# Constant tables built on chip, phi and one piece of w1 by other routes, in a fused windowed attention and soft mixture of experts

## The chip, the cores and the metric

The kernel runs on one core of a Trainium2 chip. The metric is device time in microseconds (us) of one launch. The program before was run eight times: median 183.81 us, 183.51 to 184.37. One execution was also profiled; its trace is what is read below.

## The reference

Two stages, in float32, with fixed random inputs:

```
q, k, v: (8 batches, 8 heads, 576 positions, 64)
scores = q @ k^T / 8
heads 0-3: position i sees i-31 .. i          ("plain")
heads 4-7: i sees i, i-4, i-8, .. i-124       ("dilated")
x = softmax(scores) @ v, as (4608 rows, 512 columns)

phi: (512, 32)   w1: (8, 512, 1024)   w2: (8, 1024, 512)
logits = x @ phi                               (4608, 32)
slot_input = softmax over rows(logits)^T @ x   (32, 512), 4 slots per expert
slot_out[e] = relu(slot_input[e] @ w1[e]) @ w2[e]
out = softmax over slots(logits) @ slot_out    (4608, 512)
```

The slots need all rows of x, so the second half can't begin before the attention of all batches has ended. The weights are 33.6 MB of the 62 MB that are read.

## The kernel before

The attention runs batch by batch. `prologue` (line 466) issues the first loads and clears tiles; then a loop over b runs `slot0(b)`, `slot1(b)`, `slot2(b)` (lines 528 to 601). The order inside them is the order on every engine: the whole body stands under a manual schedule, and each engine runs its instructions in that order, waiting at each for what it needs.

Loads. All big loads and all stores are issued by POOL (GpSimd)[...]. They are one queue: a load that waits for a free buffer, or a POOL copy that waits for VectorE, holds back all loads after it. q and k go to `raw` tiles (two buffers each, `load_qk`), v to `vs` tiles (`load_v`), one piece of w1 per slot to `w1t` (`load_w1`, 512 rows of an expert in two pieces, called by `weights`), and w2 near the end of the attention (`load_w2`). The program gives POOL's DMAs eight completion semaphores in turn, so the n-th DMA can't be issued before the (n-8)-th has landed.

Attention. VectorE transposes q and k out of `raw` (`qk_plain` line 237, `qk_dil` line 243). `emit_scores` (line 255) fills two PSUM tiles, `sa` and `sb`: first the bias by a product of `ident` with `masks` (line 276), then the scores on top (line 287); ScalarE takes the exponential (line 298). It runs three times a batch: g = 0 and 1 for plain heads (with the left-over part of the dilated ones in g = 1), g = 2 for the dilated ones. `order_v_plain` (line 179) brings v into row order by products with the one-hot matrices in `orders`, in the same PSUM tiles `sa` and `sb`; ScalarE copies most of it out (line 197), VectorE a small tail (line 202), and POOL and VectorE spread the dilated part (`spread_v`, lines 207 to 216). `emit_av` (line 306) multiplies with v, `emit_norm` (line 353) normalises on VectorE.

Mixture. One batch behind, `back_xT_plain`, `back_xT_dil` and `back_logits` (lines 376 to 417) transpose x, multiply with `phi4` (phi, four copies side by side) and put the exponentials into `ET`, a tile for all 4608 rows. `back_erow` and `back_u` (lines 419 to 461) sum the slot inputs into `UT`; `emask` clears rows that don't exist. After the loop: hidden layer (`hps`, line 645), its transposes (line 658), `slot_out` (line 677) for half of the 512 output columns at a time, and `combine` / `combine_full` (lines 693 and 724), which multiply `ET` with the slot outputs, scale by `rrow` on ScalarE or VectorE, and store through POOL. Experts 6 and 7 come last and in halves of columns, so that the first half of the columns can be stored while the second half of w2 is read.

Constants before: `make_masks`, `make_orders` and an identity are arrays in the program. `masks` (84 KB) and `ident` (32 KB) are read by two DMAs of SP, `orders` (128 KB) by one of POOL, all in the prologue; phi is read in rows of 32 values and copied four times by VectorE in `slot0(0)` (line 541). `slot0(0)` also clears `ET` (line 538).

Of the kernel before, what the change touches and what calls it, by code (L numbers as in the profile page):

```python
# [19 lines left out]
WINDOW = 32  # L20
DIL = 4
# [6 lines left out]
N_SLOTS = 32  # L28
FDIM = 1024
# [13 lines left out]
UNITS = 7  # L43
NH = DMODEL // 2
NSPLIT = 16


def make_masks():

    a = np.arange(128)[:, None]  # L50
    rel = np.arange(WQ)[None, :] - a
    plain = (rel >= 0) & (rel < WINDOW)
    rel = 32 + np.arange(LEFT)[None, :] - a
    left = (rel >= 0) & (rel < WINDOW) & (a < 48)
    m = [plain, plain[:, 0:TAIL]] + [left] * 5
    m = [np.where(x, 0.0, -60000.0) for x in m]
    ok = ((np.arange(128)[:, None] % 32) < LEFT) & np.ones((1, N_SLOTS), bool)
    m.append(ok)
    return np.ascontiguousarray(np.concatenate(m, axis=1).astype(np.float16))


def make_orders():

    a = np.arange(128)[:, None, None] % 32
    r = np.arange(DIL)[None, :, None]
    p = np.arange(128)[None, None, :]
    return np.ascontiguousarray((p == DIL * a + r).astype(np.float16).reshape(128, DIL * 128))


@with_exitstack  # L70
def kernel(
# [9 lines left out]
):  # L81
    nc = tc.nc

    mask_np = make_masks()
    masks_dram = nc.inline_tensor(mask_np, name="masks_d")
    orders_dram = nc.inline_tensor(make_orders(), name="orders_d")
    ident_dram = nc.inline_tensor(np.eye(128, dtype=np.float16), name="ident_d")


    consts = ctx.enter_context(tc.tile_pool(name="consts", bufs=1))  # L90
    masks = consts.tile([128, mask_np.shape[1]], FP16, name="masks")
    bias = (
        masks[:, None, 0:WQ].broadcast_to([128, 3, WQ]),
        masks[:, 0 : W1 + NLEFT],
# [57 lines left out]
    def load_qk(ti, b, groups=None):  # L152
        ten = (q, k)[ti]
        if (ti, b) not in raw:
            raw[(ti, b)] = raw_pool.tile([128, 2, PJ * D], FP16, name=f"raw{ti}_{b}", tag=f"raw{ti}")
        t = raw[(ti, b)]
        if groups is None:
            nc.gpsimd.dma_start(
                out=t, in_=ten[b].rearrange("(g h) (p j) d -> (h p) g (j d)", g=2, j=PJ)
            )  # L160
# [18 lines left out]
    def order_v_plain(b):  # L179
# [16 lines left out]
        for ab in range(2):  # L196
# [4 lines left out]
            if ab == 0:  # L201
# [2 lines left out]
                    in_=ps[0][0:TAIL, 0, 256:512].rearrange("p (h d) -> p h d", h=4),  # L204
                )

    def spread_v(b):
        sa, sb = vstage.pop(b)
        nc.vector.tensor_copy(  # L209
            out=vD[b % NV][:, :, :, 0:D], in_=sa[:, 4:8].rearrange("a h (r d) -> a h r d", r=DIL)  # L210
        )
        nc.gpsimd.tensor_copy(
            out=vL[b % NV][32 : 32 + LEFT, :, :, 0:D],
            in_=sb[0:LEFT, 4:8].rearrange("a h (r d) -> a h r d", r=DIL),
        )
        nc.gpsimd.tensor_copy(out=vL[b % NV][0:32, :, :, 0:D], in_=vD[b % NV][96:128, :, :, 0:D])  # L216

    def load_w1(e, i):
        src = moe_w1[e].rearrange("(c p) f -> p c f", p=128)
        nc.gpsimd.dma_start(out=w1t[e][:, 2 * i : 2 * i + 2, :], in_=src[:, 2 * i : 2 * i + 2, :])  # L220

    def load_w2(e, half=None):
        if half is None:
# [218 lines left out]
    def back_u(b):  # L442
        up = ring.tile([128, 5, N_SLOTS], FP32, name=f"u_{b}", tag="ring")
        er = er_t.pop(b)
        jobs = []
        for t in range(NT):
            n = 128 if t < 4 else TAIL
            for c in range(2):
                jobs.append((c, xp_t[b][0:n, t, 128 * c : 128 * c + 128], er[0:n, t, :]))
            jobs.append((4, ones[0:n, :], er[0:n, t, :]))  # L450
        for r in range(DIL + 1):
            for c in range(2):
                jobs.append((2 + c, xd_t[b][:, r, 128 * c : 128 * c + 128], er[:, NT + r, :]))
# [44 lines left out]

    def weights(b, g):
        if b < B - 2:  # L500
            if g == 1 or b > 0:
                load_w1(*next_w1.pop(0))
        elif b == B - 2:
            if g == 0:
                while next_w1:
                    load_w1(*next_w1.pop(0))
                load_w2(0)
                load_w2(1)
            else:
                slab_weights(4, "vs0", V_SLAB)  # L510
                load_w2(4)
        elif g == 0:
            raw_pool.release()
            pool = tc.alloc_tile_pool(name="w2b", bufs=1, side="right")
            late_pools.append(pool)
            for e in (2, 3):
                w2t[e] = pool.tile([128, 8, DMODEL], FP16, name=f"w2_{e}", tag=f"w2_{e}")
                load_w2(e)
        else:
            slab_weights(5, "vs1", V_SLAB)  # L520
            load_w2(5)
            slab_weights(6, "qk0", QK_SLAB)
            slab_weights(7, "v0", V_SLAB)
            for half in range(2):
                for e in HALVED:
                    load_w2(e, half)

    def slot0(b):
        att, b1, b2, b3 = b < B, b - 1 >= 0 and b <= B, 2 <= b < B + 2, b + 1 < B
        if att:  # L530
            qk_dil(1, b, 1)
            emit_scores(b, 0)
            if b + 2 < B:
                load_qk(0, b + 2)
                load_qk(1, b + 2)
            weights(b, 0)
        if b == 0:
            nc.vector.memset(ET, 0.0)
# [151 lines left out]

    psum_f = tc.alloc_tile_pool(name="psum_f", bufs=4, space=bass.MemoryType.PSUM)

    def combine(half, pair):
# [103 lines left out]
```

The softmax here doesn't subtract the row's maximum and nothing guards it: scores larger than these inputs give would overflow.

## Time and profile before

| | us |
|---|---|
| median of 8 runs | 183.81 |
| the profiled execution, its own time | 183.51 |
| its span, first to last instruction | 181.5 |
| busy: TensorE, VectorE, ScalarE, POOL | 143.8, 105.0, 89.8, 80.8 |
| 26 output DMAs, first issued at | 153.50 |

The span is shorter than the device time by about 2 us, which lie around it. Busy time of TensorE comes from matmuls that overlap, so it isn't work at full rate; the granted clock was 0.88 of full speed on average, with stretches at 0.5. In rows of the profile a line number is that of the kernel, `out<-in` are tiles, the number in front of "x" is how often; "idle before" is time in which the engine waited, and the arrow says for what. POOL's row of a DMA is only its issue; the transfer itself runs on the DMA engines.

### The profile page before, as it was taken

To read this page: it belongs to the slowest core of one execution; us is meant where nothing else is said; L and a number is where in the kernel's file an instruction comes from. 1 tells how busy PE (TensorE), PEld (TensorE's weight loads), DVE (VectorE), ACT (ScalarE), POOL (GpSimd) and SP (SyncE) were. 2 spreads that over 40 slices of the span, in tenths; PEclk is the share of its full clock that TensorE was granted. 3 is DMA by queue.
4 is the path that set the end of the run, shared out by engine and by line. 5 is a ranking of instruction groups with operands and counts; after the bars stand their busy time and mean duration, and the time that the engine had idled before them with its cause. 6 is when DMAs were issued, how large, how long until landed. Compare 5 with 4: busy or idle time off the path is not lost.

```text
span 181.5 us, 5521 instructions
## 1 busy us (share of the span) xinstructions
PE 143.8 (79%) x2448; PEld 86.8 (48%) x2448; DVE 105.0 (58%) x225; ACT 89.8 (50%) x161; POOL 80.8 (45%) x112
## 2 busy tenths in 40 slices
PE   3067989999999999999999999999879476786000
PEld 0034556557557557655746747757343253332000
DVE  2587797858767866865876976354041103599000
ACT  2044367667666765845748748745201104698000
POOL 7643644552551751541642814711101111997820
PEclk9999999999999997897899999985557967899655
DMA  5999999999999999999999999999999999999996
GB/s 81 195 205 216 197 210 205 212 209 203 213 209 203 213 210 204 211 211 201 213 209 202 212 211 211 218 213 218 212 213 215 204 195 171 335 398 409 408 408 153
DMA packets 32023, 41.00 MB, mean 226 GB/s; under 512 B 2144, under 2 KB 19680, under 8 KB 32000
## 3 DMA queue, kind: packets, MB, share of 16 engines
q0 software_dynamic: 31712, 40.54, 120.1%
q8 instruction: 19, 0.31, 0.6%
q1 hardware_dynamic: 288, 0.12, 0.3%
q14 instruction: 4, 0.03, 0.0%
HBM read 62.18 MB, written 9.44 MB: 395 GB/s over the span
## 4 chain that ended last, share of the span: by engine, by line
PE 42%; DMA 29%; issue 7%; POOL 7%; ACT 6%; DVE 3%; POOLq 0%
DMA w<-in_moe_w_dram 23%; PE lg L413 8%; PE o_p L344 7%; DMA raw<-in_q_dram 6%; PE sa L287 6%; ACT p L298 6%; PE sa L276 5%; PE sb L276 4%; PE u L455 3%; PE rd L394 2%; PE vb L188 2%; PE va L188 2%; POOL out_dram L719 2%; POOL out_dram L743 2%; PE rp L382 1%
## 5 line engine op out<-in xcount | busy, mean ns | idle before, releaser
L298 ACT ACTIVATE p<-sa 128x960 f16<-128x960 f32 (+2 forms) x24 | 21.4, 891 | 31.7 <-PE sb L287 31.1
L344 PEld LDWEIGHTS <-p 128*128 128x128 f16 (+2 forms) x544 | 19.9, 100 | 12.7 <-issue 8.6
L241 DVE STREAM_TRANSPOSE qk<-raw 128x576 uint32<-128x576 uint32 x16 | 20.0, 1250 | 5.7 <-DMA raw<-in_q_dram 4.2
L250 DVE STREAM_TRANSPOSE qk<-raw 128x320 uint32<-128x320 uint32 (+1 forms) x32 | 21.5, 677 | 0.3
L298 ACT ACTIVATE p<-sb 128x960 f16<-128x960 f32 (+2 forms) x24 | 21.2, 884 | 0.0
L216 POOL COPY v<-v 32x1024 f16<-32x1024 f16 x8 | 8.3, 1035 | 26.9 <-DVE v L209 22.2
L287 PE MATMUL sa<-qk 32*128 32x160 f16 (+4 forms) x416 | 16.0, 215 | 4.3 <-DVE qk L241 4.3
L287 PEld LDWEIGHTS <-qk 32*128 32x128 f16 x832 | 12.3, 98 | 14.2 <-issue 8.7
L413 PE MATMUL lg<-xTd,phi 128*128 128x288 f16 x32 | 18.3, 659 | 0.0
L276 PE MATMUL sa<-masks,ident 128*128 128x480 f16 (+2 forms) x48 | 14.2, 381 | 4.4 <-DMA ident<-ident_d 2.9
L344 PE MATMUL o_p<-v,p 128*128 128x65 f16 (+1 forms) x288 | 16.5, 203 | 0.7 <-ACT v L197 0.7
L232 POOL DMA_DIRECT2D w<-in_moe_w_dram x8 | 5.9, 743 | 24.9 <-DMA w<-in_moe_w_dram 20.8
L276 PEld LDWEIGHTS <-ident 128*128 128x128 f16 x96 | 9.2, 105 | 15.4 <-issue 8.7
L287 PE MATMUL sb<-qk 32*128 32x160 f16 (+4 forms) x416 | 16.1, 215 | 0.0
L276 PE MATMUL sb<-masks,ident 128*128 128x480 f16 (+2 forms) x48 | 14.6, 386 | 0.5 <-issue 0.3
L366 DVE TENSOR_TENSOR xp<-o_p,rc_p 128x448 f16<-128x448 f32 (+1 forms) x24 | 14.4, 602 | 0.8
L366 DVE TENSOR_TENSOR xd<-o_d,rc_d 128x448 f16<-128x448 f32 (+1 forms) x24 | 14.4, 602 | 0.8
L719 POOL DMA_DIRECT2D out_dram<-ot x16 | 11.3, 712 | 6.7 <-PE f L697 6.7
L220 POOL DMA_DIRECT2D w<-in_moe_w_dram x16 | 11.4, 711 | 4.4 <-DMA w<-in_moe_w_dram 2.1
L188 PE MATMUL va<-vs,orders 32*128 32x256 f16 (+1 forms) x96 | 12.1, 289 | 1.0 <-ACT p L298 1.0
L417 ACT ACTIVATE ET<-lg 128x288 f16<-128x288 f32 x16 | 6.6, 411 | 12.0 <-PE lg L413 11.8
L713 DVE TENSOR_TENSOR ot<-f,rrow 128x512 f16<-128x512 f32 x8 | 5.5, 688 | 11.9 <-PE f L697 11.8
(86 smaller groups left out, 268.0 us busy)
## 6 DMA issues: line engine op xcount, KB each, us to landing
w<-in_moe_w_dram POOLq DMA_DIRECT2D x16, 512.0 KB, 16.3
w<-in_moe_w_dram POOLq DMA_DIRECT2D x6, 1024.0 KB, 27.3
out_dram<-of POOLq DMA_DIRECT2D x10, 512.0 KB, 6.3
vs<-in_v_dram POOLq DMA_DIRECT2D x8, 512.0 KB, 13.2
out_dram<-ot POOLq DMA_DIRECT2D x16, 256.0 KB, 4.7
raw<-in_q_dram POOLq DMA_DIRECT2D x7, 576.0 KB, 14.6
raw<-in_k_dram POOLq DMA_DIRECT2D x7, 576.0 KB, 14.8
w<-in_moe_w_dram POOLq DMA_DIRECT2D x8, 256.0 KB, 23.2
```

The lines of the kernel that those rows point to most:

```text
L188: nc.tensor.matmul(o.rearrange("p (h d) -> p h d", h=4), l, st[:, 0:4, D * r : D * r + D], start=(r == 0), stop=(r == DIL - 1), skip_group ...
L216: nc.gpsimd.tensor_copy(out=vL[b % NV][0:32, :, :, 0:D], in_=vD[b % NV][96:128, :, :, 0:D])
L220: nc.gpsimd.dma_start(out=w1t[e][:, 2 * i : 2 * i + 2, :], in_=src[:, 2 * i : 2 * i + 2, :])
L241: nc.vector.transpose(out=dst, in_=src)
L250: nc.vector.transpose(out=o, in_=i)
L276: nc.tensor.matmul(sps[h // 2][:, h % 2, 0:n], ident, bias[g], start=True, stop=False, skip_group_check=True,)
L287: nc.tensor.matmul(sps[h // 2][:, h % 2, c0 : c0 + w], kt_[32 * h : 32 * h + 32, k0 : k0 + 128, tt], qt_[32 * h : 32 * h + 32, q0 : q0 + w ...
L298: nc.scalar.activation(out=pt, in_=sps[ab][:, :, 0:n], func=AF.Exp, scale=SCALE)
L344: nc.tensor.matmul(o[p0 : p0 + np_, n, :], l, rr, start=(k == 0), stop=(k == len(jobs) - 1), skip_group_check=True,)
L366: nc.vector.tensor_tensor(out=x.rearrange("p t (h d) -> p (t h) d", h=4)[0:nq, u0:u1, :], in0=o[0:nq, 0:n, 0:D], in1=rc[0:nq, 0:n, None].b ...
L413: nc.tensor.matmul(lp, phi4[:, kc].rearrange("p c s -> p (c s)"), rhs, start=(kc == 0), stop=(kc == 3))
L719: nc.gpsimd.dma_start(out=out[r0 : r0 + 256, NH * half : NH * half + NH].rearrange("(k p) n -> p k n", k=2), in_=ot,)
```

## The change

Seven edits:

1. `masks`, `ident` and `orders` are no longer read. VectorE sets `masks`, `ones` and a quarter of `orders` to constants; POOL cuts them to shape with affine selects, five after v's first load and one, for `orders`, after q of batch 1. VectorE copies the tail part of `masks` (ahead of the first `qk_plain`) and three quarters of `orders` (ahead of the first `qk_dil`).
2. `emask`'s last block comes from a row sum over `orders` instead of a column block of `masks`.
3. phi is read as 128 rows of 512 bytes, later in POOL's queue, and put in order by 16 one-hot products in batch 1 (`order_phi`), in the PSUM tiles of the scores; ScalarE copies the four-fold result to `phi4`.
4. Each piece of w1 is read as two neighbouring rows a partition (8 KB in one run) instead of two rows 128 apart. `back_u` takes every second column of x, so that slot inputs match.
5. 64 partitions of the first piece of w1 are read as float32 by SP and ACT, 8 DMAs of 8 partitions, into a part of `ET` that is still unused (`side_load`); POOL casts them to their place in `slot0(0)` (`side_cast`), and `ET` is cleared after it. POOL's own load of that piece has only the other 64 partitions.
6. Two pieces of w1 are issued in the prologue and one in `slot0(0)`, where there was none; later pieces move up.
7. The first pair of output blocks of half 0 is stored block by block (`combine_one`).

```diff
@@ kernel head
-    mask_np = make_masks()
-    masks_dram = nc.inline_tensor(mask_np, name="masks_d")
-    orders_dram = nc.inline_tensor(make_orders(), name="orders_d")
-    ident_dram = nc.inline_tensor(np.eye(128, dtype=np.float16), name="ident_d")
...
+    def order_phi():
+        ps = [psum_s.tile([128, 2, 512], FP32, name=f"phi{ab}", tag=f"s{ab}") for ab in "ab"]
+        for r in range(DIL):
+            for c in range(4):
+                nc.tensor.matmul(
+                    ps[c // 2][:, c % 2, 0:128].rearrange("p (u s) -> p u s", u=4),
+                    orders[32 * c : 32 * c + 32, r, :],
+                    phi_raw[32 * c : 32 * c + 32, r, None, :].broadcast_to([32, 4, N_SLOTS]),
+                    start=(r == 0),
+                    stop=(r == DIL - 1),
+                    skip_group_check=True,
+                )
+        for ab in range(2):
+            nc.scalar.copy(
+                out=phi4[:, 2 * ab : 2 * ab + 2].rearrange("p c u s -> p c (u s)"),
+                in_=ps[ab][:, :, 0:128],
+            )
...
+    SIDE_P = 64
+    side = ET[0:SIDE_P, 0 : 4 * FDIM].bitcast(FP32)
+
+    def side_load():
+        src = moe_w1[0, 0:256].rearrange("(p l) f -> p (l f)", l=2)
+        for n, p in enumerate(range(0, SIDE_P, 8)):
+            (nc.sync, nc.scalar)[n % 2].dma_start(out=side[p : p + 8], in_=src[p : p + 8])
+
+    def side_cast():
+        nc.gpsimd.tensor_copy(
+            out=w1t[0][0:SIDE_P, 0:2, :].rearrange("p l f -> p (l f)"), in_=side
+        )
+
     def load_w1(e, i):
-        src = moe_w1[e].rearrange("(c p) f -> p c f", p=128)
-        nc.gpsimd.dma_start(out=w1t[e][:, 2 * i : 2 * i + 2, :], in_=src[:, 2 * i : 2 * i + 2, :])
+        p0 = SIDE_P if (e, i) == (0, 0) else 0
+        nc.gpsimd.dma_start(
+            out=w1t[e][p0:128, 2 * i : 2 * i + 2, :].rearrange("p l f -> p (l f)"),
+            in_=moe_w1[e, 256 * i : 256 * i + 256].rearrange("(p l) f -> p (l f)", l=2)[p0:128],
+        )
@@ back_u
-                jobs.append((c, xp_t[b][0:n, t, 128 * c : 128 * c + 128], er[0:n, t, :]))
+                x = xp_t[b][0:n, t, :].rearrange("p (x l) -> p l x", l=2)
+                jobs.append((c, x[:, c, :], er[0:n, t, :]))
...
@@ prologue
         load_qk(0, 0, (0,))
         load_qk(1, 0, (0,))
-        nc.sync.dma_start(out=masks, in_=masks_dram.ap())
-        nc.sync.dma_start(out=ident, in_=ident_dram.ap())
+        side_load()
+        nc.vector.memset(masks, 0.0)
+        nc.vector.memset(ones, 1.0)
+        nc.vector.memset(orders[0:32], 1.0)
...
         load_qk(0, 0, (1,))
         load_qk(1, 0, (1,))
-        nc.gpsimd.dma_start(out=orders.rearrange("p r n -> p (r n)"), in_=orders_dram.ap())
         load_v(0)
-        nc.gpsimd.dma_start(out=phi_raw, in_=moe_phi.rearrange("(c p) s -> p c s", p=128))
+        left = masks[:, W1:].rearrange("p (u c) -> p u c", c=LEFT)
+        band = (
+            (ident, ones, [[1, 128]], 0, -1, ALU.is_equal, 0.0),
+            (masks[:, 0:WQ], masks[:, 0:WQ], [[1, WQ]], 0, -1, ALU.is_ge, MASKED),
+            (masks[:, 0:WQ], masks[:, 0:WQ], [[-1, WQ]], WINDOW - 1, 1, ALU.is_ge, MASKED),
+            (left, left, [[0, 5], [1, LEFT]], 32, -1, ALU.is_ge, MASKED),
+            (left, left, [[0, 5], [-1, LEFT]], -1, 1, ALU.is_ge, MASKED),
+        )
+        for dst, src, pattern, base, mult, op, fill in band:
+            nc.gpsimd.affine_select(
...
         load_qk(0, 1)
+        nc.gpsimd.affine_select(
+            out=orders[0:32],
...
         load_qk(1, 1)
         load_v(1)
+        nc.gpsimd.dma_start(out=phi_raw, in_=moe_phi.rearrange("(p l) s -> p l s", l=4))
+        for _ in range(2):
+            load_w1(*next_w1.pop(0))
+        nc.vector.tensor_copy(out=masks[:, WQ:W1], in_=masks[:, 0:TAIL])
         qk_plain(0, 0)
         qk_plain(1, 0)
-        nc.vector.memset(ones, 1.0)
         nc.vector.memset(emask, 1.0)
+        for i in range(1, 4):
+            nc.vector.tensor_copy(out=orders[32 * i : 32 * i + 32], in_=orders[0:32])
@@ weights
         if b < B - 2:
-            if g == 1 or b > 0:
-                load_w1(*next_w1.pop(0))
+            load_w1(*next_w1.pop(0))
@@ slot0
         if b == 0:
+            side_cast()
             nc.vector.memset(ET, 0.0)
             nc.vector.memset(siTm, 0.0)
-            nc.vector.tensor_copy(out=emask[:, NE - 1, :], in_=masks[:, W1 + NLEFT :])
+            nc.vector.tensor_reduce(
+                out=halves, in_=orders[:, 0, 0:TAIL], axis=mybir.AxisListType.X, op=ALU.add
+            )
             nc.vector.tensor_copy(
-                out=phi4, in_=phi_raw[:, :, None, :].broadcast_to([128, 4, 4, N_SLOTS])
+                out=emask[:, NE - 1, :], in_=halves.broadcast_to([128, N_SLOTS])
             )
...
         if att and b > 0:
             order_v_plain(b)
+        if b == 1:
+            order_phi()
...
+    def combine_one(half, blk):
+        fp = psum_f.tile([128, NH], FP32, name=f"f{half}_one{blk}", tag="f")
+        cols = slice(NH * half, NH * half + NH)
+        r0 = 128 * blk
+        nc.tensor.matmul(fp, ET[:, r0 : r0 + 128], so_sb[:, cols], start=True, stop=True)
+        ot = out_pool.tile([128, NH], FP16, name=f"oo{half}_{blk}", tag=f"oo{half}_{blk}")
+        if blk % 2 == 0:
+            nc.scalar.activation(out=ot, in_=fp, func=AF.Copy, scale=rrow[:, blk : blk + 1])
+        else:
+            nc.vector.tensor_scalar(
+                out=ot, in0=fp, scalar1=rrow[:, blk : blk + 1], scalar2=None, op0=ALU.mult
+            )
+        nc.gpsimd.dma_start(out=out[r0 : r0 + 128, cols], in_=ot)
+
     def combine(half, pair):
+        if half == 0 and pair == 0:
+            combine_one(half, 0)
+            combine_one(half, 1)
+            return
```

More of the change, by code (lines that the diff above doesn't have):

```diff
@@ L43 @@
 UNITS = 7
+MASKED = -60000.0
 NH = DMODEL // 2
 NSPLIT = 16
[L48 to L67, printed above, removed]
 @with_exitstack
@@ L82 @@
     nc = tc.nc
-    mask_np = make_masks()
-    masks_dram = nc.inline_tensor(mask_np, name="masks_d")
-    orders_dram = nc.inline_tensor(make_orders(), name="orders_d")
-    ident_dram = nc.inline_tensor(np.eye(128, dtype=np.float16), name="ident_d")
     consts = ctx.enter_context(tc.tile_pool(name="consts", bufs=1))
-    masks = consts.tile([128, mask_np.shape[1]], FP16, name="masks")
+    masks = consts.tile([128, W1 + NLEFT], FP16, name="masks")
+    halves = consts.tile([128, 1], FP32, name="halves")
     bias = (
@@ L452, in back_u @@
             for c in range(2):
-                jobs.append((2 + c, xd_t[b][:, r, 128 * c : 128 * c + 128], er[:, NT + r, :]))
+                x = xd_t[b][:, r, :].rearrange("p (x l) -> p l x", l=2)
+                jobs.append((2 + c, x[:, c, :], er[:, NT + r, :]))
         for i, (c, l, rr) in enumerate(jobs):
@@ L480, in prologue @@
         load_qk(1, 0, (1,))
-        nc.gpsimd.dma_start(out=orders.rearrange("p r n -> p (r n)"), in_=orders_dram.ap())
         load_v(0)
-        nc.gpsimd.dma_start(out=phi_raw, in_=moe_phi.rearrange("(c p) s -> p c s", p=128))
-        load_qk(0, 1)
+        left = masks[:, W1:].rearrange("p (u c) -> p u c", c=LEFT)
[8 more added lines that the diff above has]
+            nc.gpsimd.affine_select(
+                out=dst,
+                in_=src,
+                pattern=pattern,
+                base=base,
+                channel_multiplier=mult,
+                compare_op=op,
+                fill=fill,
+            )
+        load_qk(0, 1)
+        nc.gpsimd.affine_select(
+            out=orders[0:32],
+            in_=orders[0:32],
+            pattern=[[-1, DIL], [1, 128]],
+            base=0,
+            channel_multiplier=-DIL,
+            compare_op=ALU.is_equal,
+            fill=0.0,
+        )
         load_qk(1, 1)
         load_v(1)
+        nc.gpsimd.dma_start(out=phi_raw, in_=moe_phi.rearrange("(p l) s -> p l s", l=4))
+        for _ in range(2):
+            load_w1(*next_w1.pop(0))
+        nc.vector.tensor_copy(out=masks[:, WQ:W1], in_=masks[:, 0:TAIL])
         qk_plain(0, 0)
         qk_plain(1, 0)
-        nc.vector.memset(ones, 1.0)
         nc.vector.memset(emask, 1.0)
+        for i in range(1, 4):
+            nc.vector.tensor_copy(out=orders[32 * i : 32 * i + 32], in_=orders[0:32])
         for part in range(2):
@@ L537, in slot0 @@
         if b == 0:
+            side_cast()
             nc.vector.memset(ET, 0.0)
             nc.vector.memset(siTm, 0.0)
-            nc.vector.tensor_copy(out=emask[:, NE - 1, :], in_=masks[:, W1 + NLEFT :])
+            nc.vector.tensor_reduce(
+                out=halves, in_=orders[:, 0, 0:TAIL], axis=mybir.AxisListType.X, op=ALU.add
+            )
             nc.vector.tensor_copy(
-                out=phi4, in_=phi_raw[:, :, None, :].broadcast_to([128, 4, 4, N_SLOTS])
+                out=emask[:, NE - 1, :], in_=halves.broadcast_to([128, N_SLOTS])
             )
@@ L691 @@
     psum_f = tc.alloc_tile_pool(name="psum_f", bufs=4, space=bass.MemoryType.PSUM)
+    def combine_one(half, blk):
[9 more added lines that the diff above has]
+                out=ot, in0=fp, scalar1=rrow[:, blk : blk + 1], scalar2=None, op0=ALU.mult
+            )
+        nc.gpsimd.dma_start(out=out[r0 : r0 + 128, cols], in_=ot)
     def combine(half, pair):
+        if half == 0 and pair == 0:
+            combine_one(half, 0)
+            combine_one(half, 1)
+            return
         fp = psum_f.tile([128, 2, NH], FP32, name=f"f{half}_{pair}", tag="f")
```

## The prediction

> **What bounds the kernel now.** I read the page first: the slices by time, the DMA queues, the chain of waits.
>
> ```profile
> DMA  5999999999999999999999999999999999999996
> GB/s 81 195 205 216 197 210 205 212 209 203 213 209 203 213 210 204 211 211 201 213 209 202 212 211 211 218 213 218 212 213 215 204 195 171 335 398 409 408 408 153
> HBM read 62.18 MB, written 9.44 MB: 395 GB/s over the span
> ```
>
> GB/s counts bytes written. Loads are float32 cast to float16, so 207 written is about 414 read, the same flow as the output's 408. The transfers never rest between about 4 and 179 us, so bytes alone set a floor for the span. But the second limit is close. One-microsecond windows (span, then busy PE, PEld, DVE, ACT, POOL, then clock, DMA share, GB/s) show a slow start and, in the middle, a TensorE with no idle time:
>
> ```profile
> 2.00:3.00 1.00, 0.14 (x1) 0.13 (x2) 0.31 (x3) 0.02 (x1) 1.00 (x2) 1.00 0.81 105
> 3.00:4.00 1.00, 1.00 (x3) 0.30 (x2) 0.00 (x0) 0.00 (x0) 1.00 (x3) 1.00 0.77 115
> ...
> 61.00:62.00 1.00, 1.00 (x4) 0.26 (x3) 0.97 (x3) 1.00 (x2) 0.49 (x1) 1.00 1.11 218
> ```
>
> So attention, at about 13.7 us a batch, can't catch up on a late start. How late may it be? I went to the timeline of the tail (start, length, what; idle before it in brackets):
>
> ```profile
> 141.93 1.17 PE L681 MATMUL so<-w,hTm 128*32 128x256 f16 x36 [0.38 <-DVE hTm L662]
> 145.79 3.38 PE L681 MATMUL so<-w,hTm 128*32 128x256 f16 x64 [2.69 <-DMA w<-in_moe_w_dram]
> 149.81 0.29 PE L681 MATMUL so<-w,hTm 128*32 128x256 f16 x4 [0.65 <-DMA w<-in_moe_w_dram]
> 151.13 0.29 PE L681 MATMUL so<-w,hTm 128*32 128x256 f16 x4 [1.02 <-DMA w<-in_moe_w_dram]
> 153.50 4.91 POOL L719 DMA_DIRECT2D out_dram<-ot  x7 [6.73 <-PE f L697]
> ```
>
> These waits are the whole slack between compute and weights: 2.69 + 0.65 + 1.02 = 4.36 us. A compute chain later by more starts the output later by the rest. Last, the timeline of the start, for what starts the attention:
>
> ```profile
> 4.94 0.59 POOL L175 DMA_DIRECT2D vs<-in_v_dram  x1
> 5.71 1.26 DVE L241 STREAM_TRANSPOSE qk<-raw 128x576 uint32<-128x576 uint32 x1 [3.29 <-DMA raw<-in_q_dram]
> 7.85 0.71 POOL L158 DMA_DIRECT2D raw<-in_k_dram  x1 [0.85 <-DMA raw<-in_k_dram]
> 9.23 2.55 DVE L250 STREAM_TRANSPOSE qk<-raw 128x320 uint32<-128x320 uint32 x4
> 12.20 2.00 DVE L538 MEMSET ET<- 128x2336 uint32 x1 [0.41 <-issue]
> 16.77 1.25 DVE L241 STREAM_TRANSPOSE qk<-raw 128x576 uint32<-128x576 uint32 x1 [0.95 <-DMA raw<-in_q_dram]
> 17.87 0.40 DVE L202 CAST v<-va 64x256 f16<-64x256 f32 x1
> 18.32 1.01 PE L276 MATMUL sa<-masks,ident 128*128 128x512 f16 x2 [0.24 <-DVE v L202]
> 20.23 1.25 DVE L241 STREAM_TRANSPOSE qk<-raw 128x576 uint32<-128x576 uint32 x1 [0.86 <-DMA raw<-in_k_dram]
> ```
>
> VectorE runs these in order. The third group of scores of batch 0 (18.32) needs the small v copy (17.87), which stands behind the memset of ET. The bracket at 7.85 shows POOL's issue limit: the n-th of its DMAs waits until the eighth before it has landed (k1, the tenth, for k0, the second).
>
> [...]
>
> **The change, part by part.**
>
> Bytes. The orders load goes: 131 KB of float16 at 414 GB/s, 0.3 us. Masks and ident (116 KB) landed before 2.9 us, when the engines were not full: nothing. phi falls from 512 to 128 packets; its landing leaves no dip that v's rows don't explain, so 0.1 us (0 to 0.5). w1 in rows of 8 KB: before, 104 to 112 us, w1's 4 KB rows, flowed at 211, and 112 to 120 us, mostly w2's 8 KB rows, at 216; 8.39 MB written at each differ by 0.9 us, and as the stretches are mixed I take 0.5 (0 to 0.9). The side load: half a megabyte into the slow start. The windows from 2 to 6 us (105, 115, 171, 171 of 210) lack 1.3 us of flow, and half a megabyte takes 1.2 us on all engines. [...] I take 0.3 (0 to 1.2). Sum about 1.2 us of floor.
>
> The split first output. Now the first output DMA is issued 2.08 us after the last product of half 0 (151.42 to 153.50). One block in place of two saves a product and one ScalarE scaling of about 0.4: 0.6 us.
>
> Stride-2 operands in the slot inputs: the same 25 products a batch. The tail's products on stride-4 columns load weights in 114 ns against 96 for packed ones; at most 20 x 18 ns a batch, hidden by pipelining, so nothing (0 to 2 us over 8 batches).
>
> POOL's start. Without orders, v's second piece is issued by 5.0 us. [...] Five selects, 608 columns: POOL's copies take 1035 ns for 1024 columns, so 0.6 us at that rate, twice it with starts: 1.2 (0.8 to 2), until 12.2. Behind them wait q1, k1, v1, phi, two w1 loads, q2, k2. With q0, k0 and v0 written (1.77 MB) and the side load, the engines run dry near 12: some 1.5 us of flow lost.
>
> VectorE's start. The copy of the mask's tail stands ahead of the first transposes, so these begin at 12.3 rather than 5.71: two at 1.25, then memset 0.3, three copies of orders 0.6, four dilated transposes 2.6: until 18.3 (11.8 before). The first bias products lie beside that. First scores come near 14.8 instead of 8.9.
>
> The new wait. The side load's tile is in ET. VectorE's memset of ET must wait for POOL's cast of it, and that cast is behind the third w1 DMA, whose issue waits until k1 has landed. k1 is issued near 14.4; q1 and k1 together are 1.18 MB, 5.7 us at 207 from about 13.5 on, and v1 is mixed in, so it lands near 20. Issue 0.7, cast of 2048 columns at the copy's rate 2.07: until 22.8. Memset 2.0, siTm and two small ones 0.7, transpose 1.25, v copy 0.4: 27.2 instead of 18.3, 8.9 us late. [...] So the wait decides[...]. Behind the memset stand all of VectorE's norms and q1's transposes.
>
> order_phi: 16 narrow products in batch 1 wait for both v copies, and the next scores for the two ScalarE copies: v's copy freed the bank at 28.5; products 0.5[...], copies 0.7: 1.5 us (0.5 to 2). Removing phi's 1.13 us VectorE copy at 14.69 gains nothing behind a later wait.
>
> Sum: compute is X = 8.9 + 1.5 = 10.4 us late. Without DMA waits the last product of half 0 ends at 151.42 - 4.36 + X = 147.06 + X. First output 1.48 later (2.08 - 0.6). The output is 9.44 MB at 408, 23.1 us, and 1.0 from issue to flow, then 2.85 from the last byte (178.65) to the end of the span: 175.5 + X = 185.9, against 181.5: +4.4. Against the profiled execution's 183.51 this is 187.9; the median of the runs is 0.3 above that execution: **188.2 us**. The floor saved by fewer bytes is not lost time any more: the weights arrive before they are asked for.
>
> **Rivals.**
>
> A: the slack covers it. If X stays under 5.8, the transfers remain the bound, and the end moves by the bytes and the earlier output: -1.2 - 0.3, 182.3 us. For it: TensorE's clock is 0.5 from 122 to 138, and at full clock the 5.67 us of hidden-layer products would be 2 us shorter; the loop's waits for POOL and VectorE may give some back. Against it: [...] X is 8.5. It decides where the ET wait costs under about 4 us.
>
> B: [...] puts k1, the cast and everything behind 6 us later: X = 16, 194 us; the DMA engines would be empty from 12 to 19. [...]
>
> C: [...] the ET wait as worked out: X = 8.5, 186.3 us. This belongs to my forecast's range.
>
> **How the numbers follow.** Forecast, C included, from 184.5 to 190.5: 0.68. A: 0.15, of it 0.11 faster and 0.04 within 0.2%. B: 0.17. A measurement of this kernel can't tell under 0.2% (0.37 us) from no change. Chances: faster 0.11, same 0.04, slower 0.85. Range: from 183.7, which leaves out most of A, to 193.0, which leaves out the far part of B: about 0.18 outside.
>
> **What would show it.** The memset of ET starts near 22.8 with idle time put down to POOL; first transposes near 12.3, behind POOL's selects; third scores of batch 0 near 27; flow dips between 12 and 14; the chain of waits has little w2 DMA and more TensorE; the flow falls for some 3 us between the last w2 and the output, near 157 to 160. The forecast is wrong if [...] the cast of the side load runs before 16 us, or if the waits for w2 in the tail stay as long as they are.

## The result, and the profile after

| | before | after |
|---|---|---|
| median, us | 183.96 (32 runs, 183.41 to 184.73) | 192.96 (11 runs, 189.64 to 193.88) |
| profiled execution, us | 183.51 | 193.86 |
| its span, us | 181.5 | 192.0 |

The changed kernel takes 1.0388 times as long (95% interval 1.0358 to 1.0419). The ratio counts fast runs alone, 5 of the changed kernel's 11 (median 191.42 us), so it is smaller than the quotient of the medians; the profiled execution is one of the slow ones.

The page of the kernel after: busy share of the DMA engines and bytes written in 40 slices, two of the DMA queues (packets, MB, share of 16 engines' span), the bytes of HBM, and the shares of the chain that ended last.

```profile
DMA  5999999999999999999999999999999997999994
GB/s 81 145 192 206 207 202 214 183 211 214 200 208 215 141 194 210 178 207 213 172 208 211 180 200 213 215 213 213 217 215 209 198 196 96 256 390 407 406 411 98
...
q1 hardware_dynamic: 64, 0.26, 1.0%
q10 hardware_dynamic: 64, 0.26, 0.9%
...
HBM read 61.93 MB, written 9.44 MB: 372 GB/s over the span
...
PE 59%; ACT 8%; DMA 8%; POOL 7%; issue 7%; DVE 6%; POOLq 1%; DVEq 0%; ACTq 0%
```

The shares of the chain before:

```profile
PE 42%; DMA 29%; issue 7%; POOL 7%; ACT 6%; DVE 3%; POOLq 0%
```

Before, the flow was level until the last weights; now it is low in the second slice (145 against 195), has hollows in the loop (141, 178, 172, 180) and falls to 96 between the weights and the output. In the chain the share of DMA fell from 29% to 8%, and that of TensorE rose from 42% to 59%. The kernel has gone from bound by bytes to bound by a late compute chain. Note the DMA row: it shows 9 in the second slice in both kernels, and the engines that count as busy there moved 145 GB/s in this one and 195 in the one before.

The timeline of the start, kernel after (start, length, what; in brackets the idle time before, and what ended it):

```profile
0.81 1.59 ACTq L216 DMA_DIRECT2D ET<-in_moe_w_dram  x4
0.81 1.37 SPq L216 DMA_DIRECT2D ET<-in_moe_w_dram  x4
...
5.18 0.29 POOL L503 TENSOR_SCALAR_AFFINE_SELECT ident<-ones 128x128 f16<-128x128 f16 x1
5.43 1.29 POOL L503 TENSOR_SCALAR_AFFINE_SELECT masks<-masks 128x160 f16<-128x160 f16 x4
6.17 0.24 DVE L527 COPY masks<-masks 128x64 f16<-128x64 f16 x1 [2.85 <-POOL masks L503]
...
8.01 0.74 POOL L132 DMA_DIRECT2D raw<-in_k_dram  x1
11.64 2.34 DVE L249 STREAM_TRANSPOSE qk<-raw 128x576 uint32<-128x576 uint32 x2 [5.23 <-DMA raw<-in_q_dram]
11.90 0.89 POOL L146 DMA_DIRECT2D vs<-in_v_dram  x1 [3.15 <-DMA raw<-in_q_dram]
...
24.47 0.56 POOL L225 DMA_DIRECT2D w<-in_moe_w_dram  x1 [2.11 <-DMA raw<-in_k_dram]
25.03 1.90 POOL L219 CAST w<-ET 64x2048 f16<-64x2048 f32 x1
27.48 2.00 DVE L580 MEMSET ET<- 128x2336 uint32 x1 [9.65 <-POOL w L219]
31.33 0.40 DVE L176 CAST v<-va 64x256 f16<-64x256 f32 x1
31.78 1.01 PE L284 MATMUL sa<-masks,ident 128*128 128x512 f16 x2 [8.58 <-DVE v L176]
```

Two things are to be seen. First, VectorE is ready at 6.4 and waits 5.23 us for q, and POOL waits 3.15 us for the same landing; before, q was there at 5.71. The five selects are over by 6.7, five microseconds before q lands, so they aren't what the attention waits for. Second, k of batch 1, issued at 8.01, has landed only at 24.4. POOL's third w1 DMA waits for that, the cast stands behind it, VectorE's clearing of `ET` waits 9.65 us for the cast, and the third scores of batch 0 come at 31.78 instead of 18.32: 13.46 us late.

Two-microsecond windows of the start, kernel after (span, busy PE, PEld, DVE, ACT, POOL, then clock, DMA share, GB/s):

```profile
2.00:4.00 2.00, 0.00 (x0) 0.00 (x0) 0.92 (x11) 1.28 (x1) 2.00 (x5) 1.00 0.62 90
4.00:6.00 2.00, 0.00 (x0) 0.10 (x1) 0.00 (x0) 0.00 (x0) 1.81 (x5) 1.00 1.08 154
6.00:8.00 2.00, 1.76 (x4) 0.41 (x3) 0.24 (x1) 0.00 (x0) 1.93 (x5) 1.00 1.26 153
8.00:10.00 2.00, 0.00 (x0) 0.00 (x0) 0.00 (x0) 0.00 (x0) 0.75 (x2) 1.00 1.02 147
```

The same view of the kernel before, from 4 us on:

```profile
4.00:6.00 2.00, 0.64 (x2) 0.00 (x0) 0.29 (x1) 0.00 (x0) 2.00 (x4) 1.00 1.06 171
6.00:8.00 2.00, 0.00 (x0) 0.00 (x0) 1.37 (x2) 0.00 (x0) 1.15 (x3) 1.00 1.10 205
8.00:10.00 2.00, 0.99 (x24) 0.77 (x25) 1.94 (x5) 0.07 (x1) 1.32 (x2) 1.00 1.13 228
```

From 4 to 10 us the flow stays at 150 GB/s, where before had 171, 205 and 228, though POOL had issued q, k and v of batch 0 by 5.1. And nearly half of what was written from 2 to 10 us (1.09 MB) is the side load's own half megabyte. The tail, kernel after, timeline:

```profile
150.75 5.79 PE L691 MATMUL hps<-w,siTm 128*32 128x512 f16 x64 [1.06 <-DVE siTm L677]
...
158.40 3.13 PE L727 MATMUL so<-w,hTm 128*32 128x256 f16 x108 [0.39 <-DVE hTm L708]
161.58 0.37 ACT L735 CAST so_sb<-so 128x256 f16<-128x256 f32 x1 [2.83 <-PE so L727]
...
163.07 1.09 POOL L751 DMA_DIRECT2D out_dram<-oo  x2 [9.77 <-DVE oo L748]
```

The hidden layer of the kernel before:

```profile
134.40 5.67 PE L645 MATMUL hps<-w,siTm 128*32 128x512 f16 x64 [1.05 <-DVE siTm L631]
```

In these two executions the hidden layer starts 16.35 us later than before. The 4.36 us of waits for w2 are gone: 108 products run in one go, because the weights lie there already. The first output is issued 9.57 us later (153.50 before), and the end is 10.5 us later.

### The profile page after: what moved, and what is told of

The parts are those of the page before. It is cut to its first block, busy times and chain, and to the rows that moved or that the text cites. A ratio compares the mean times of both kernels' runs of the same rounds, so it can differ in the third digit from the quotient of the medians.

```text
span 192.0 us, 5600 instructions
## 1 busy us (share of the span) xinstructions
PE 142.5 (74%) x2464; PEld 86.1 (45%) x2464; DVE 106.0 (55%) x232; ACT 90.3 (47%) x162; POOL 82.5 (43%) x119
## 2 busy tenths in 40 slices
DMA packets 29336, 41.02 MB, mean 214 GB/s; under 512 B 1664, under 2 KB 19072, under 8 KB 29248
## 3 DMA queue, kind: packets, MB, share of 16 engines
q0 software_dynamic: 29184, 40.15, 112.3%
## 4 chain that ended last, share of the span: by engine, by line
PE 59%; ACT 8%; DMA 8%; POOL 7%; issue 7%; DVE 6%; POOLq 1%; DVEq 0%; ACTq 0%
PE lg L421 11%; DMA raw<-in_q_dram 8%; PE o_p L352 7%; ACT p L306 6%; PE sa L295 6%; PE sa L284 5%; PE sb L284 5%; PE u L465 4%; PE rd L402 3%; PE hps L691 3%; PE rp L390 2%; PE vb L162 2%; PE va L162 2%; POOL out_dram L783 2%; PE so L727 2%
## 5 line engine op out<-in xcount | busy, mean ns | idle before, releaser
L284 PE MATMUL sa<-masks,ident 128*128 128x480 f16 (+2 forms) x48 | 15.1, 402 | 15.8 <-DVE v L176 8.6
L284 PE MATMUL sb<-masks,ident 128*128 128x480 f16 (+2 forms) x48 | 15.2, 403 | 0.2 <-ACT p L306 0.2
L425 ACT ACTIVATE ET<-lg 128x288 f16<-128x288 f32 x16 | 6.6, 411 | 12.3 <-PE lg L421 12.2
L240 POOL DMA_DIRECT2D w<-in_moe_w_dram x8 | 5.9, 744 | 14.5 <-DMA w<-in_moe_w_dram 14.5
L373 DVE RECIPROCAL rc_p<-o_p 128x7 f32<-128x7 f32 (+1 forms) x24 | 4.7, 197 | 12.4 <-PE o_p L352 11.9
L395 ACT COPY xTp<-rp 128x576 f16<-128x576 f16 x16 | 10.4, 648 | 2.2 <-PE rp L390 2.1
L225 POOL DMA_DIRECT2D w<-in_moe_w_dram x16 | 8.9, 559 | 5.1 <-DMA raw<-in_k_dram 3.0
```

Source lines behind the costliest of these rows:

```text
L225: nc.gpsimd.dma_start(out=w1t[e][p0:128, 2 * i : 2 * i + 2, :].rearrange("p l f -> p (l f)"), in_=moe_w1[e, 256 * i : 256 * i + 256].rearr ...
L284: nc.tensor.matmul(sps[h // 2][:, h % 2, 0:n], ident, bias[g], start=True, stop=False, skip_group_check=True,)
L395: nc.scalar.copy(out=xTp_t[b][:, c, :], in_=rg)
```

## The experiments

Unless said otherwise, each kernel is the changed one with the edit shown. "Wait" is short for VectorE's clearing of `ET` waiting for POOL's cast.

**No side load.** POOL reads the whole first piece of w1 itself.

```diff
-        side_load()
-            side_cast()
-        p0 = SIDE_P if (e, i) == (0, 0) else 0
+        p0 = 0
```

> Changed kernel without the side load: POOL reads the whole first piece of w1, nothing is cast, the memset of ET waits for nothing. Theory W (the wait of ET's memset for the cast is the cost; the side load's own flow is harmless) and theory P (the 8-partition side loads hold up q0 and k0, and k1 behind them) agree here: q0 lands near 6 us as before, the first transposes start by 7, the third scores of batch 0 start at 18 to 19.5, order_phi still costs 1.6, the lateness of about 2 to 3 us is under the slack of 4.4: 182.5 to 184.5 us. A rival (the affine selects or the w1 pieces moved up are the cost) expects over 187.

Measured: 184.0 us, ratio 1.0003 (0.9985 to 1.0021). Timeline of this kernel:

```profile
18.04 1.03 PE L284 MATMUL sa<-masks,ident 128*128 128x512 f16 x2
```

Third scores at 18.04 and hidden layer at 134.23 are close to before (18.32 and 134.40). All of the loss hangs on the side load; the other edits together come to nothing. Some of them turn out below to cancel.

**The same eight DMAs, other partitions.** Each takes eight partitions four apart instead of eight neighbours.

```diff
-        for n, p in enumerate(range(0, SIDE_P, 8)):
-            (nc.sync, nc.scalar)[n % 2].dma_start(out=side[p : p + 8], in_=src[p : p + 8])
+        for n, p in enumerate((0, 1, 2, 3, 32, 33, 34, 35)):
+            rows = slice(p, p + 29, 4)
+            (nc.sync, nc.scalar)[n % 2].dma_start(out=side[rows], in_=src[rows])
```

> Same eight side loads of 8 partitions, but each takes every fourth partition (b, b+4, .. b+28) instead of eight neighbours: same bytes, rows, queues [...]. Theory P [...]: q0 lands near 7 to 8 us instead of 11.6, k1 near 19 to 20 instead of 24.4, the memset of ET starts near 22 to 23, time 185.5 to 188.5. [...] theory W: q0 stays at 11 to 12, memset of ET near 27, time 189.5 to 193.5.

Measured: 191.36 us, ratio 1.0375 (1.0313 to 1.0437). The time lies where theory W expected it (189.5 to 193.5); only the start follows theory P. The page's queue and the timeline of this kernel:

```profile
q1 hardware_dynamic: 64, 0.26, 0.5%
```

```profile
0.81 3.66 ACTq L217 DMA_DIRECT2D ET<-in_moe_w_dram  x4
0.81 2.78 SPq L217 DMA_DIRECT2D ET<-in_moe_w_dram  x4
...
9.99 1.26 DVE L250 STREAM_TRANSPOSE qk<-raw 128x576 uint32<-128x576 uint32 x1 [2.45 <-DMA raw<-in_k_dram]
...
21.95 0.56 POOL L226 DMA_DIRECT2D w<-in_moe_w_dram  x1 [1.88 <-DMA raw<-in_k_dram]
...
24.96 2.00 DVE L581 MEMSET ET<- 128x2336 uint32 x1 [9.78 <-POOL w L220]
```

The engines spent half the time on the same bytes: 0.5% of 16 engines over 189.8 us is 15.2 us for SP's queue, against 1.0% over 192.0 us, 30.7 us, in the changed kernel. The flow from 2 to 10 us is back (150, 160, 224, 226), and q is there by 6.3. The edit changed more than the partitions: the rows of w1 that one DMA reads no longer lie together, and the DMAs were issued more slowly, ACT's four in 3.66 us against 1.59 and SP's in 2.78 against 1.37, which may have left q's load more room. Neither was tried alone. It is shown, then, that the start recovers when the partitions are spread, with the rows and the pace that come with it; which of the three is the reason isn't shown.

Yet the end hardly moved: k of batch 0 still landed late (9.99), k of batch 1 at 21.9, and the wait ended at 24.96, 1.8 us later than in the next kernel. From the third scores to the hidden layer this kernel then took 119.6 us, the next one 116.1. From 45 to 75 us its granted clock was 0.84, that of the next kernel 1.00; whether this made the 3.5 us isn't settled.

**Two DMAs of 64 partitions.** Half the columns each.

```diff
-        for n, p in enumerate(range(0, SIDE_P, 8)):
-            (nc.sync, nc.scalar)[n % 2].dma_start(out=side[p : p + 8], in_=src[p : p + 8])
+        for n in range(2):
+            cols = slice(FDIM * n, FDIM * n + FDIM)
+            (nc.sync, nc.scalar)[n].dma_start(out=side[:, cols], in_=src[0:SIDE_P, cols])
```

> Side load as two DMAs of 64 partitions (half of the columns each), one from SP and one from ACT. [...] about as the spread 8-partition loads, q0 at 7 to 8, 185.5 to 188.5 us. [...] this one alone is fast, q0 near 7, and the spread one is not. Theory W: no change, 189.5 to 193.5.

Measured: 187.44 us, ratio 1.0213 (1.0148 to 1.0278). Timeline of this kernel:

```profile
7.13 2.64 DVE L250 STREAM_TRANSPOSE qk<-raw 128x576 uint32<-128x576 uint32 x2 [0.72 <-DMA raw<-in_q_dram]
...
23.16 2.00 DVE L581 MEMSET ET<- 128x2336 uint32 x1 [9.36 <-POOL w L220]
...
27.46 1.01 PE L285 MATMUL sa<-masks,ident 128*128 128x512 f16 x2 [8.32 <-DVE v L176]
```

Now q is there at 7.1 and k before VectorE asks for it, and the flow is 245, 173, 209, 200 in the four windows. With the transfer repaired, the wait is left alone: 187.44 less 183.88, 3.6 us, from four runs between 186.75 and 189.35.

**No wait.** The narrow side load stays; VectorE clears only the part of `ET` that doesn't hold it, and the few cells beneath it that must be zero (32 partitions, seven times 64 columns) later, in batch 1.

```diff
-            nc.vector.memset(ET, 0.0)
+            nc.vector.memset(ET[:, 4 * FDIM :], 0.0)
...
             order_phi()
+            over = ET[0:32, S : B * S].rearrange("p (b c) -> p b c", c=S)
+            nc.vector.memset(over[:, :, 0:64], 0.0)
```

> Side load and cast as in the changed kernel, but VectorE clears only the part of ET behind the side load's columns at once; the few columns that are read before they are written are cleared in batch 1. So nothing on VectorE waits for the cast. Theory W: the third scores start near 22 to 24 us instead of 31.8 (q0 is still late), lateness with order_phi 6 to 8, time 184.5 to 187. Theory P alone (the wait is only a follower of the late q0 and k1): third scores at 29 or later, 189 or more.

Measured: 186.64 us, ratio 1.0157 (1.0121 to 1.0193). Timeline of this kernel:

```profile
9.16 1.26 DVE L249 STREAM_TRANSPOSE qk<-raw 128x576 uint32<-128x576 uint32 x1 [2.74 <-DMA raw<-in_q_dram]
...
16.92 0.30 DVE L580 MEMSET ET<- 128x288 uint32 x1
...
22.21 1.03 PE L284 MATMUL sa<-masks,ident 128*128 128x512 f16 x2
...
151.90 0.29 PE L729 MATMUL so<-w,hTm 128*32 128x256 f16 x4 [1.04 <-DMA w<-in_moe_w_dram]
```

Third scores 3.9 us late, which the slack covers: the waits for w2 in the tail are back (the row shown is one of three). This kernel is bound by its bytes again. It lacks 2.8 us against before and 2.9 against the next kernel. In its first 20 us it moved 170 GB/s, the next one 185: about 1.4 us of flow. Where the rest arises isn't fully traced; from 154 to 156 us, before the output, its flow falls to 77 GB/s, where the next kernel's lowest is 179. Note that q landed at 9.16 here and at 11.64 in the changed kernel, with the same side load: beside the narrow transfers it was 3.5 us late in the one execution and 5.9 in the other.

**Both repairs.** The edits of the last two kernels together: two wide DMAs and no wait. This is called the repaired kernel below.

> Changed kernel with both costs of the side load taken away: two DMAs of 64 partitions in place of eight of 8, and ET's memset no longer behind the cast (early part cleared at once, a few columns in batch 1). If the side load's shape (flow at the start) and the wait are the whole loss, the third scores of batch 0 start at 18 to 19.5 us and the time is that of the kernel without the side load or up to 1 us below it, 183.0 to 184.2. If the moved w1 loads or the cast on POOL cost something of their own: 184.5 to 186.

Measured: 183.72 us, ratio 1.0002 (0.9991 to 1.0014); third scores at 18.82. The four kernels make a square: the wait alone costs 2.1%, the narrow shape alone 1.6%, both 3.9%, neither nothing. The two causes nearly add, and together they are the loss. That they add isn't a matter of course. Alone, the narrow load costs bytes; beside the wait it also makes the wait end later, 27.48 instead of 23.16, because k lands later (k of batch 1 at 24.4 instead of 20.1).

**What the rest is worth.** Three kernels take single edits apart. No side load, and phi as before:

```diff
-        if b == 1:
-            order_phi()
...
-        nc.gpsimd.dma_start(out=phi_raw, in_=moe_phi.rearrange("(p l) s -> p l s", l=4))
+        nc.gpsimd.dma_start(out=phi_raw, in_=moe_phi.rearrange("(c p) s -> p c s", p=128))
...
+            nc.vector.tensor_copy(
+                out=phi4, in_=phi_raw[:, :, None, :].broadcast_to([128, 4, 4, N_SLOTS])
+            )
```

> Changed kernel without the side load and with phi as before (rows of 128 bytes, four-fold copy on VectorE, no one-hot products). If order_phi's 1.6 us on the attention chain matter at the end, this is 0.5 to 1.6 us faster than the version without the side load (184.0): 182.4 to 183.5. If the slack in front of the last w2 covers them: 183.6 to 184.4, no difference.

Measured: 184.33 us, 1.0039 (1.0020 to 1.0058): nothing is gained by taking the one-hot products out. Its hidden layer began at 142.06 in the one trace there is, of an execution of 185.84 us, with several slices at a granted clock of 0.5 to 0.9; why is open.

The kernel before, with 8 KB rows of w1 and every second column of x:

```diff
-        nc.gpsimd.dma_start(out=w1t[e][:, 2 * i : 2 * i + 2, :], in_=src[:, 2 * i : 2 * i + 2, :])
+        nc.gpsimd.dma_start(
+            out=w1t[e][:, 2 * i : 2 * i + 2, :].rearrange("p l f -> p (l f)"),
+            in_=moe_w1[e, 256 * i : 256 * i + 256].rearrange("(p l) f -> p (l f)", l=2),
+        )
...
-                jobs.append((c, xp_t[b][0:n, t, 128 * c : 128 * c + 128], er[0:n, t, :]))
+                x = xp_t[b][0:n, t, :].rearrange("p (x l) -> p l x", l=2)
+                jobs.append((c, x[:, c, :], er[0:n, t, :]))
```

> Kernel before with one edit alone: w1 read as two neighbouring rows a partition (8 KB runs), and the slot inputs with every second column. The prediction's term is 0.5 us less floor: 183.0 to 183.5. If run length above 4 KB doesn't matter: 183.7 to 184.1. If the stride-2 operands cost: over 184.3.

Measured: 184.54 us, 1.0047 (1.0029 to 1.0065), half a per cent slower, although by 140 us it had written 28.82 MB against 28.70, which is 0.6 us ahead.

The kernel before, with the first two output blocks stored one by one, `combine_one` as in the change:

```diff
     def combine(half, pair):
+        if half == 0 and pair == 0:
+            combine_one(half, 0)
+            combine_one(half, 1)
+            return
```

> Kernel before with one edit alone: the first pair of output blocks stored block by block. The prediction's term is 0.6 us less: 183.0 to 183.4. If the stores are held by the DMA engines, which still have w2 to read, an earlier issue gains nothing: 183.7 to 184.1.

Measured: 183.56 us, 0.9990 (0.9976 to 1.0003). Timeline of this kernel:

```profile
151.87 0.37 ACT L689 CAST so_sb<-so 128x256 f16<-128x256 f32 x1 [12.74 <-PE so L681]
...
153.36 1.09 POOL L705 DMA_DIRECT2D out_dram<-oo  x2 [6.21 <-DVE oo L702]
```

From the copy of the slot output to the first issue 1.49 us, 2.03 before: 0.54 saved, and the end hardly notices.

**Where the gain of the bytes went.** The repaired kernel should have been ahead: the last output landed 1.3 us sooner (SP goes on at 179.1, before at 180.4). Its span is the same, 181.5. The DRAIN instructions at the end of the program show where the gain went. Rows of the repaired kernel (duration shortest/median/longest in ns, then first and last start in us; the longest of POOL's is the first):

```profile
L859 POOLq DRAIN  x3: 51/91/9152, 171.6 to 181.2; - x3
L859 SPq DRAIN  x3: 7/7/7, 179.1 to 181.0; - x3
```

SP's first drain starts when the last output has landed: its queue's wait before is put down to an output DMA. POOL's long drain ends at 171.6 + 9.15 = 180.75, 1.65 us after that; before, it ended 0.4 us after. Three kernels were made to find what it depends on. The repaired one with w1 in 4 KB rows again and plain columns (the rows of the side load and the second list of operands follow; they aren't shown here):

```diff
+        src = moe_w1[e].rearrange("(c p) f -> p c f", p=128)
         nc.gpsimd.dma_start(
-            out=w1t[e][p0:128, 2 * i : 2 * i + 2, :].rearrange("p l f -> p (l f)"),
-            in_=moe_w1[e, 256 * i : 256 * i + 256].rearrange("(p l) f -> p (l f)", l=2)[p0:128],
+            out=w1t[e][p0:128, 2 * i : 2 * i + 2, :], in_=src[p0:128, 2 * i : 2 * i + 2, :]
         )
...
-                x = xp_t[b][0:n, t, :].rearrange("p (x l) -> p l x", l=2)
-                jobs.append((c, x[:, c, :], er[0:n, t, :]))
+                jobs.append((c, xp_t[b][0:n, t, 128 * c : 128 * c + 128], er[0:n, t, :]))
```

> Wide side load and split clearing of ET, but w1 in 4 KB rows and plain columns as before (change 4 taken out). In every traced version with 8 KB rows, POOL's last drain, from the last output issue to the end of POOL's program, takes 9.0 to 9.3 us, against 7.86 in the two versions with 4 KB rows. Theory (the long drain comes with the 8 KB rows): drain 7.9, the flow loses the 0.6 us gained by the rows, end 183.0 (182.6 to 183.4), ratio 0.993 to 0.998. Rival (the long drain comes with the other edits, or varies by itself): drain 9.2, end 184.3, ratio 1.003.

Measured: 182.74 us, 0.9939 (0.9915 to 0.9963).

The kernel before with 8 KB rows alone, which is the first part of the diff of the kernel before with 8 KB rows above, without its columns:

> Kernel before with w1 in 8 KB rows alone; columns of x stay packed, so the slot inputs are multiplied with w1 rows in another order (the mixture's result is left wrong). Theory (8 KB rows make the drain long): drain 9.2, 184.5, as with the strided columns. Rival (the strided columns or the code of TensorE make it): drain 7.9, 183.2.

Measured: 184.75 us, 1.0047 (1.0031 to 1.0064): the rows do it, not the columns.

The first experiment's edit (no side load) and 4 KB rows together:

> The change without the side load and without 8 KB rows. Theory: drain 7.9, and 184.0 less 1.3 plus 0.6 gives 183.3, ratio 0.997 (0.994 to 0.999). Rival: 184.6, ratio 1.004.

Measured: 182.94 us, 0.9947 (0.9923 to 0.9970).

Last, the fastest so far with the second piece of every expert in 8 KB rows and the first in 4 KB rows:

```diff
+        if i == 1:
+            nc.gpsimd.dma_start(
+                out=w1t[e][:, 2:4, :].rearrange("p l f -> p (l f)"),
+                in_=moe_w1[e, 256:512].rearrange("(p l) f -> p (l f)", l=2),
+            )
+            return
```

> The fastest version so far (wide side load, split clearing, 4 KB rows: 182.74 us, POOL's last drain 7.72 us) with the second piece of w1 of every expert in 8 KB rows, the first in 4 KB rows. Theory 1 (the drain grows with the number of 8 KB DMAs or falls with the number of packets, evenly): drain near 8.4, end 183.1. Theory 2 (one such DMA is enough, or a threshold below half): drain 9.2, end 183.8, as with all pieces. Theory 3 (a threshold above half, or where the last DMAs land): drain 7.7, the flow gains 0.3, end 182.5.

Measured: 182.22 us, 0.9913 (0.9889 to 0.9937): the lowest of all medians, 0.9% under the kernel before; its lead over 4 KB rows alone (0.9939) lies within the intervals. The same rows of the kernel before, of the kernel before with 8 KB rows, of the repaired kernel with 4 KB rows, and of the last one:

```profile
L792 POOLq DRAIN  x3: 51/91/7856, 172.9 to 181.2; - x3
L792 SPq DRAIN  x3: 7/7/7, 180.4 to 181.0; - x3
```

```profile
L796 POOLq DRAIN  x3: 51/91/9290, 172.5 to 182.2; - x3
L796 SPq DRAIN  x3: 7/7/7, 180.0 to 182.0; - x3
```

```profile
L856 POOLq DRAIN  x3: 51/91/7717, 171.9 to 180.1; - x3
L856 SPq DRAIN  x3: 7/7/7, 179.5 to 179.9; - x3
```

```profile
L863 POOLq DRAIN  x3: 51/91/7430, 171.8 to 179.7; - x3
L863 SPq DRAIN  x3: 7/7/7, 179.2 to 179.5; - x3
```

In the first, third and fourth kernel POOL's drain ends within 0.4 us of the last landing (172.9 + 7.86 = 180.8 against 180.4); in the second 1.8 us after it (172.5 + 9.29 = 181.8 against 180.0), and the program ends only then. All traced kernels fall into these two kinds (those not in the table have 8 KB rows and 1.6 to 1.8 us):

| kernels | packets of POOL's queue | drain ends after the landing, us |
|---|---|---|
| before; before with split output | 31,712; 31,728 | 0.4; 0.3 |
| 4 KB rows: repaired; no side load | 31,168; 31,296 | 0.1; 0.2 |
| half in 8 KB rows | 30,144 | 0.0 |
| before with 8 KB rows, strided; packed | 29,664; 29,664 | 1.8; 1.7 |
| changed; both repairs; no side load | 29,184; 29,184; 29,248 | 1.65; 1.65; 1.7 |

It isn't an even growth with the number of long rows (half of them cost nothing), nor does one such DMA suffice. Whether the packets count, the rows, or which pieces are long can't be told from these runs.

## Why the prediction held, and where its steps failed

The forecast of 188.2 us had the direction and the chief mechanism right: the wait of `ET` outgrows the slack. The size was too small, 4.4 us foreseen against 9.0 between the medians and 7.1 by the ratio. The median, 192.96, lies just inside the range (to 193.0), but above the 184.5 to 190.5 of the forecast itself, in the stretch that was left to rival B. So the range held partly by luck. Step by step:

- **The side load in the bytes: the step that failed.** It was priced at 0.3 us (0 to 1.2), by its bytes. That its narrow DMAs would hold up the loads beside them wasn't thought of. It cost q's landing 5.9 us (11.64 instead of 5.71), k of batch 1 some 4.3 us (24.4, against 20.1 with the wide load), and 2.8 us of the end even without the wait.
- **A pause of POOL ahead of the first select: it didn't happen.** The prediction has POOL's issues end at 5.0 us and five selects of 1.2 us end at 12.2. The pause between them was the author's assumption and isn't shown by any trace. The first select began 0.1 us after POOL's last issue (5.18 against 5.07). The five selects took 1.55 us, inside the 0.8 to 2 given.
- **First transposes at 12.3: right time, wrong cause.** They began at 11.64, but behind a DMA, not behind the selects. Two errors, a pause that did not come and a transfer that was 5.9 us late, stood in for each other.
- **The wait of the clearing of `ET`: right from k's landing on.** Third scores were foreseen at 27.2 from k's landing near 20, and came at 31.78 as k landed at 24.4. With the wide load k landed at 20.1, the clearing began at 23.16 (22.8 foreseen), and the scores at 27.46. But the 20 was luck too: it was reached through the pause. The prediction's own row of the kernel before, 20.23, shows k of batch 1 landing at 20.2 although it had been issued at 7.85. With the wide load and no pause, which is rival C's case, the scores were 9.1 us late where its 8.5, less 1.5 for `order_phi`, has 7.
- **`order_phi` 1.5 us: right in place, without effect.** The last v products ahead of it come 13.41 us later than in the kernel before (40.21 against 26.80), the first scores behind it 14.99 later (43.54 against 28.55): 1.6 more. It stands in the compute chain, and with the slack there its removal gained nothing (184.33 us).
- **Slack of 4.36 us: right**; the waits for w2 vanished in the kernels whose third scores came 9 us late or more, and stayed in the one where they came 3.9 late.
- **From there to the end.** 10.4 us was foreseen for the hidden layer and 16.35 measured: 4.6 of the difference were there at the third scores, the other 1.4 came in the loop. From there to the hidden layer the changed kernel took 119.0 us, the one before 116.1 and the one with the wide load 116.1, so that it was not `order_phi`, which the last of these has too. From 45 to 75 us its granted clock was 0.84, where before had 0.94 (1.00 to 60 us, 0.89 after it). Its time went with the clock as a whole: 189.64 us at a mean of 0.931, 193.88 at 0.895. That the clock made the difference is argued, not shown. The 12.3 us from there to the first output are 1.8 shorter than the sum (14.1), since the 108 products ran in one go, in 3.13 us, at a granted clock of 1.00 from 157 to 162 us; before, 64 of them took 3.38, at 0.55 to 0.60 from 145 to 149. The output's last part is 2.0 longer (28.9 against 26.95), of which 1.3 is POOL's long drain. 185.9 + 5.95 - 1.8 + 1.95 = 192.0, the span of the profiled execution.
- **Floor of bytes, 1.2 us, and split output, 0.6 us: right in size, not in worth.** The last landing did come 1.3 us sooner in the repaired kernel, and the issue 0.54 sooner; the first was given back in the drain, the second moved the end by 0.1%, which can't be told from nothing (-0.24% to +0.03%).
- **Stride-2 columns at nothing: right**, 184.54 us with and 184.75 without them.

Rival A (the slack covers it) was excluded for the right reason: the wait costs more than the slack. Rival B had nearly the time (194 us), by a longer pause of POOL, which no trace shows. Of the signs named beforehand, the clearing's idle time put down to POOL and the missing waits for w2 appeared; the gap before the output came at 158 to 163 us; the flow fell not near 12 to 14 but from 4 to 11 us.

## What to carry to other kernels

Price a small transfer by its shape and by what it delays, not by its bytes alone: half a megabyte at the start of a kernel that is bound by transfers held up everything the first compute needed (q at 11.64 us instead of 5.71), and as two wide DMAs it did little harm (7.13). A borrowed buffer brings a wait for its return, and the return stands behind everything that is queued on the engine that copies it out (9.65 us of idle time before the clearing here); clear only what isn't lent. And where a saving shows in the last landing but not in the span, read the rows of the program's end before giving the saving up: here, half of the row edit was worth more than all of it (182.22 us against 183.72).

## What the runs showed of the hardware

- Eight DMAs of 64 KB, each on eight neighbouring partitions, kept the engines busy for 30.7 us in SP's queue, and for 15.2 us on eight partitions four apart. Beside the neighbouring ones the first q landed 3.5 to 5.9 us later than before (9.16 and 11.64 against 5.71). The views counted the engines as busy meanwhile (DMA share of 1.02 to 1.26 from 4 to 10 us).
- The first affine select on POOL started 0.1 us after a DMA issue, without a wait of its own: 0.29 us for 128 x 128 float16, 1.29 us for the four on the mask tile.
- POOL's final drain ended up to 0.4 us, or 1.6 to 1.8 us, after the last landing, depending on the format in which w1 had been loaded, long before.
